# Output products of 13 tiles of layer 1 put off to the end of the kernel

## The chip, the cores and the metric

The kernel runs on one core of a Trainium2 chip. The metric is the time of one execution on the device in microseconds (us); lower is better. "PE" is the matrix engine (TensorE), "DVE" the vector engine, "ACT" the scalar engine, "POOL" GpSimd and "SP" the engine whose queue issues the DMAs.

## What is computed

The input is x, 2048 rows of 512 numbers in float32. Two kinds of layer alternate, twice each:

```python
x = x + A(layernorm(x)); x = x + B(layernorm(x))      # layer 0 of the kernel
x = x + A(layernorm(x)); x = x + B(layernorm(x))      # layer 1 of the kernel

def A(x):   # Fourier mixing: real part of a transform over features and rows
    a, b = x @ dft_hid_re.T, x @ dft_hid_im.T
    return dft_seq_re @ a - dft_seq_im @ b            # 2048 x 2048 matrices

def B(x):   # experts looked up by product keys: 32 heads, 16 + 16 keys, 256 experts
    q = einsum("nd,dhc->nhc", x, w_q)
    s1, s2 = q[..., :128] @ k1.T, q[..., 128:] @ k2.T # 16 scores each, per head
    # the best 2 of each, the best 2 of their 4 sums: 2 experts e with gates g (softmax)
    act = gelu(einsum("nd,nhkd->nhk", x, u[e]))
    return einsum("nhk,nhk,nhkd->nd", g, act, v[e])
```

## The kernel before

**Layout.** The 2048 rows are 16 tiles of 128. Float32 products are made exact enough by splitting each operand into a rounded high part and the remaining low part (`xh` and `xl` for the normalized x), so that one product is three matmuls: high by high, high by low, low by high.

**Stages.** Each layer has nine units of rows: units 0 to 6 have two tiles each, units 7 and 8 one tile. `ORDER` lists them; in layer 1 it is 0, 7, 1, 2, 3, 4, 5, 6, 8. For each unit, `seq_unit` (matmuls of L510) multiplies all 16 blocks of normalized x by that unit's blocks of the row transform. The blocks come by DMA (`raw`, L446), are split by ACT (L450) and DVE (L454), and the sum of the 16 steps lies in four accumulators `acc`. The sum is split into `pth` and `ptl` (L535, L538). The mark `xfree[s]` is the last use of block s of x.

Then `token_tile` works through each tile of the unit:

- the feature transform (L607), the add of the row (L617) and the layernorm;
- turning the normalized row over. For the tiles marked by `MOVED` (the first 13 of layer 1 among them), DVE turns 32x32 blocks (L659), the result goes to DRAM (L663), and four DMAs bring back pieces with the blocks in turned order, in runs of 32 numbers (L672). For other tiles PE transposes (L691);
- the scores (L721, L725) and the products with all 256 rows of u (L752);
- top-two selection by chains of maximum and comparison on DVE (L811 to L916), for 32 heads at a time;
- the gates, built as a 128 x 256 matrix: comparisons on DVE (L956, L962), small matmuls (L972), an ACT copy (L982), out to DRAM in four DMAs (`gdr`, L1002) and back in two (`gt` or, for the last tile, `raw`, L1010), because the values change partitions on the way;
- p, the product of gates and gelu (L1012). PE turns p (L1020), ACT and DVE split it into `ph` and `pl` (L1024, L1028), and six matmuls of 128x512 multiply it by the 256 rows of v, `vh` and `vl` (L1039, L1043). DVE adds the result to the row (L1054), and SP stores the row (L1059 in layer 1).

**What sets the order.** All this is written as operations given to a planner (`Plan`). Each has an engine, an assumed duration, its predecessors, the buffers that it takes (`take`) and gives back (`last`), and a priority. The planner takes operations in order of the time at which they could start, and among those that could start first the one with the lowest priority tuple. The operations are then issued in order of planned start, so that the order on each engine is fixed. Token work (priority 0) comes before sequence products (priority 5). For the last tile (tile 15, unit 8; `FINAL`, `fine`) an operation is also preferred when it could start within `SLACK` = 0.14 us of the first. A DMA is planned with at most eight (`LANES`) on the way. On SP the planner takes 0.3 us for one of the four turned pieces and 1.05 us for 256 KB.

When the last sequence product has been planned and a gap on PE of over 1.0 us remains, filler matmuls whose result isn't used are put into it (L1123).

```python
            elif free >= seq_last.start and gap > 1.0:
                for _ in range(int((gap - 0.4) / MM512)):
                    fill(1)
```

The functions that the diff touches:

Of the kernel before, what the change touches and what calls it, by code (L numbers as in the profile page):

```python
# [8 lines left out]
F32 = mybir.dt.float32  # L9
F32R = mybir.dt.float32r  # L10
# [18 lines left out]
E = 16  # L29
N = E * E  # L30
# [13 lines left out]
def MOVED(layer, at):  # L44
    return at >= 2 if layer == 0 else at < NCH + NSC * (TPC - 1) - 2


FILL0 = 10
FIRST = 4
LANES = 8  # L50
# [19 lines left out]
class Plan:  # L70
# [77 lines left out]
MM512, MM256, TR32, TR16, MMG = 0.230, 0.121, 0.110, 0.057, 0.026  # L148


def dve(n, rate=1):
    return 0.069 + n / (0.96e3 * rate)


def act(n):
    return 0.09 + n / 1.2e3


def load(kb):
    return kb / 256 * 1.05  # L160
# [3 lines left out]
def spectral_peer_kernel(ctx: ExitStack, tc, x_in, cseq, ctile, dhid, wq, k1t, k2t, ut, vm, out):  # L164
    nc = tc.nc
# [6 lines left out]


    BUFS = {"acc": 4, "bank": 4, "raw": 4, "c": 3, "p": 1, "row": 4, "wr": 5, "wp": 2,
            "tok": 3, "sc": 1, "eq": 1, "act": 3, "q": 2, "top": 1, "qt": 1, "lr": 4, "gt": 1, "pp": 1, "gdr": 2, "xdr": 2, "bn": 1}
    plan = Plan(BUFS)


    xh = const.tile([P, NT, D], F32R, name="xh")
    xl = const.tile([P, NT, D], F32R, name="xl")  # L180
    dh = const.tile([P, 2, KD, D], F32R, name="dh")
    dl = const.tile([P, 2, KD, D], F32R, name="dl")
    wh = const.tile([P, KD, 2, H, E], F32R, name="wh")
# [3 lines left out]
    vh = const.tile([P, 2, D], F32R, name="vh")  # L187
# [74 lines left out]
    def ln_apply(dst, src, i):  # L262
        nc.scalar.activation(dst, src, AF.Identity, bias=stats[:, i, 2:3], scale=stats[:, i, 1:2])
# [5 lines left out]

    def xhat(layer, i, get, after, take, last, prio):  # L270
        if layer == 0 and i < FIRST:
            b = xhigh[i] = op("ACT", act(512) + 0.18, lambda: ln_apply(xh[:, i, :], get(), i), after, take=take, prio=prio)
            a = op("ACT", act(512) + 0.18, lambda: ln_apply(get(), get(), i), [b], prio=prio)
            xready[layer, i] = op("DVE", dve(512), lambda: nc.vector.tensor_sub(xl[:, i, :], get(), as32(xh[:, i, :])),
                                  [a], last=last, prio=prio)
            return
        a = op("ACT", act(512) + 0.18, lambda: ln_apply(get(), get(), i), after, take=take, prio=prio)
        b = op("ACT", act(512), lambda: nc.scalar.copy(xh[:, i, :], get()), [a], prio=prio)
        xready[layer, i] = op("DVE", dve(512), lambda: nc.vector.tensor_sub(xl[:, i, :], get(), as32(xh[:, i, :])),
                              [b], last=last, prio=prio)  # L280

    xload = {}
# [143 lines left out]
    def seq_unit(layer, at, n, banks="acc"):  # L426
# [42 lines left out]
        def target(d):  # L469
            if b is None:  # L470
                return acc[d].rearrange("p c t -> p (c t)")
            return acc[d // 2][:, d % 2]

        for s0 in range(0, NT, 2):
            for s in (s0, s0 + 1):
                if s % per == 0:
                    pieces[s // per] = piece(s // per)

            steps = [(d, s) for s in (s0, s0 + 1) for d in range(KD)]
            if layer == 0 and at == 0 and s0 < FIRST:  # L480

                for s in (s0, s0 + 1):
                    ready, hc, moving = pieces[s]

                    def f(s=s, moving=moving, parts=(0, 1)):
                        for d in range(KD):
                            if s == 0:
                                acc[d] = psum.tile([P, 2, T], F32, name=banks, bufs=BUFS[banks])
                            for part in parts:
                                nc.tensor.matmul(target(d), xh[:, s, d * P:(d + 1) * P], moving(0, part),  # L490
                                                 start=(s == 0 and part == 0), stop=False, skip_group_check=True)

                    def g(s=s, moving=moving):
                        for d in range(KD):
                            nc.tensor.matmul(target(d), xl[:, s, d * P:(d + 1) * P], moving(0, 0),
                                             start=False, stop=False, skip_group_check=True)

                    seq_last = op("PE", 2 * KD * MM512, f, [ready, xhigh[s], seq_last], take=hold if s == 0 else [], prio=rank)
                    seq_last = xfree[s] = op("PE", KD * MM512, g, [xready[layer, s], seq_last], last=[hc], prio=rank)
                yield  # L500
                continue
            for d, s in sorted(steps) if s0 == NT - 2 else steps:
                ready, hc, moving = pieces[s // per]

                def f(s=s, d=d, moving=moving):
                    if s == 0 and d % blocks == 0:
                        shape = [P, 2, T] if b is None else [P, 2, 2, P]
                        acc[d // blocks] = psum.tile(shape, F32, name=banks, bufs=BUFS[banks])
                    for k, (w, part) in enumerate(((xh, 0), (xl, 0), (xh, 1))):
                        nc.tensor.matmul(target(d), w[:, s, d * P:(d + 1) * P], moving(s % per, part),  # L510
                                         start=(s == 0 and k == 0 and d % blocks == 0),
                                         stop=(s == NT - 1 and k == 2), skip_group_check=True)

                final = d == KD - 1 and s % per == per - 1
                seq_last = op("PE", 3 * (MM512 if b is None else MM256), f,
                              [ready, xready[layer, s], seq_last],
                              take=[hold[d // blocks]] if s == 0 and d % blocks == 0 else [],
                              last=[hc] if final else [], prio=rank)
                if d == KD - 1:
                    xfree[s] = seq_last  # L520
                    if s == NT - 4:
                        near[layer, n] = seq_last
                done[d] = seq_last
            yield
# [24 lines left out]
                parts[d] = firsts[-1], a  # L549


    x2done = {}
    last = {}
    stores = []
# [2 lines left out]
    def token_tile(layer, n, i, t0, at):  # L557
# [2 lines left out]
        late = (0, layer, at, i, 1)  # L560
        fine = prio[:3] == FINAL
        moved = MOVED(layer, at)
        hrow = Hold("row")
        t = {}

# [60 lines left out]
            a = ln_stats(lambda: t["row"], i, [b] + ([xready[1, i]] if (1, i) in xready else []), prio)  # L626


        hx, hxb = Hold("tok"), Hold("lr")
        ks = [slice(0, KD)] if not fine else [slice(0, KD // 2), slice(KD // 2, KD)]  # L630
        xn = []

        def f_xn(z, k):
            def f():
                if z == 0:
                    t["xn"] = work([P, D], F32, "tok")
                cs = slice(k.start * P, k.stop * P)
                if z == 0:
                    ln_apply(t["xn"][:, cs], t["row"][:, cs], i)
                else:  # L640
                    nc.vector.tensor_scalar(t["xn"][:, cs], t["row"][:, cs], stats[:, i, 1:2], stats[:, i, 2:3],
                                            op0=ALU.mult, op1=ALU.add)
            return f

        for z, k in enumerate(ks):
            w = (k.stop - k.start) * P
            xn.append(op("DVE", dve(w), f_xn(z, k), [a], behind=xn, prio=prio) if z else
                      op("ACT", act(w) + 0.18, f_xn(z, k), [a] + setup_done, take=[hx], prio=prio))

        hth, htl = Hold("tok"), Hold("tok")  # L650
        a_th, a_tl = [], []
# [354 lines left out]
        for j in range(2):  # L1006
            def f_in(j=j):
# [2 lines left out]
                nc.sync.dma_start(t["gt"][j * 64:(j + 1) * 64], t["gdr"][j].rearrange("e t g f -> (t g) e f"))  # L1010
            back.append(op("SP", 0.4, f_in, moves, behind=back, take=[hgt] if j == 0 else [], last=[hd], prio=prio, lag=3.5))
        a = op("DVE", dve(N), lambda: nc.vector.tensor_mul(t["act"], t["act"], t["gt"].rearrange("p e f -> p (e f)")),  # L1012
               back + [a_act], last=[hgt], prio=prio)

        hb, hpp = Hold("bank"), Hold("pp")

        def f_pt():
            t["pt"] = bank([P, 2, P])
# [1 line left out]
                nc.tensor.transpose(t["pt"][:, k, :], t["act"][:, k * P:(k + 1) * P], identf)  # L1020

        def f_ph():
            t["ph"] = work([P, 2, P], F32R, "ph", "pp")
            nc.scalar.copy(t["ph"], t["pt"])  # L1024

        def f_pl():
            t["pl"] = work([P, 2, P], F32R, "pl", "pp")
            nc.vector.tensor_sub(t["pl"], t["pt"], as32(t["ph"]))  # L1028

        a = op("PE", 2 * TR32, f_pt, [a], take=[hb], last=[hact], prio=prio)  # L1030
# [76 lines left out]

    for layer in range(2):
        mix(layer)

    order = sorted(plan.run(), key=lambda o: o.start)

# [64 lines left out]
```

## Time and profile before

| | |
|---|---|
| median of 3 runs | 1273.01 us (1272.3 to 1273.83) |
| the profiled execution, its own time | 1273.94 us |
| its span, first to last instruction | 1272.2 us |
| busy PE / DVE / ACT / POOL | 98% / 79% / 37% / 4% of the span |
| mean granted PE clock | 0.998 of full speed |
| moved by DMA | 134.55 MB, mean 106 GB/s |

The profiled execution is one run; its time contains about 1.7 us around the span. Times in the rows of the profile are microseconds from the span's start. A matmul's duration contains its way through the array and overlaps the next one's, so a PE that is 98% busy is not at its peak; how close two matmuls follow each other is read from the chain that ended last, in order of time. "Idle before, released by" names what an instruction had waited for.

### The profile page before, as it was taken

What the parts mean: (1) busy time and instruction counts of PE and PEld (TensorE: products, weight loads), DVE (VectorE), ACT (ScalarE), POOL (GpSimd) and SP (SyncE); (2) the same over time, 40 slices, a digit from 0 to 9 for tenths busy, and PEclk for the clock granted to TensorE, in tenths of its full rate; (3) what the DMA queues carried; (4) which work ended last, traced back from release to release, by engine and by line L of the source; (5) the groups of instructions that cost most, each with busy time, mean ns of one, the idle gap of its engine ahead of it and who ended that gap; (6) DMA issues with size and microseconds to landing.
All of it is one profiled execution on the core that took longest, in us unless ns stands there. A gap on an engine that the chain in (4) does not pass through costs nothing.

```text
span 1272.2 us, 20722 instructions
## 1 busy us (share of the span) xinstructions
PE 1251.6 (98%) x7686; PEld 1033.4 (81%) x7686; DVE 1007.7 (79%) x2277; ACT 466.6 (37%) x968; POOL 46.7 (4%) x71
## 2 busy tenths in 40 slices
PE   9999999999999999999999999999999999999997
PEld 6877778777787888899889887887888888888985
DVE  8899998899896877769885498595686849686784
ACT  7522143343333333334563233333333333333411
POOL 2000000000100000000000000000000000000000
PEclk9999999999999999999999999999999999999999
DMA  7866540342525242442554223424243342424002
GB/s 237 270 193 212 191 150 27 86 102 69 117 66 120 80 91 80 100 113 72 134 151 134 82 67 90 109 67 119 73 99 101 83 116 74 116 59 100 26 10 42
DMA packets 284693, 134.55 MB, mean 106 GB/s; under 512 B 193840, under 2 KB 259888, under 8 KB 284592
## 3 DMA queue, kind: packets, MB, share of 16 engines
q1 hardware_dynamic: 284592, 133.23, 39.1%
q8 instruction: 60, 0.98, 0.3%
q14 instruction: 41, 0.34, 0.1%
HBM read 114.05 MB, written 19.14 MB: 105 GB/s over the span
## 4 chain that ended last, share of the span: by engine, by line
PE 71%; DVE 14%; issue 5%; DMA 5%; ACT 2%; SPq 2%; POOL 1%; POOLq 0%; DVEq 0%; ACTq 0%
PE acc L510 40%; PE bank L607 10%; PE bank L721 7%; PE bank L725 3%; PE bank L752 3%; PE bank L1039 2%; DVE cl L454 2%; PE bank L510 2%; PE bank L384 1%; DMA tok<-xdr 1%; DVE eq L805 1%; DVE w L376 1%; DMA raw<-x2d 1%; PE bank L972 1%; PE bank L1043 1%
## 5 line engine op out<-in xcount | busy, mean ns | idle before, releaser
L510 PE MATMUL acc<-ch,xh 128*128 128x512 f32 (+1 forms) x1072 | 405.7, 378 | 0.2 <-DVE ptl L538 0.2
L510 PE MATMUL acc<-cl,xh 128*128 128x512 f32 (+1 forms) x1072 | 397.6, 371 | 0.0
L510 PE MATMUL acc<-ch,xl 128*128 128x512 f32 (+1 forms) x1072 | 397.4, 371 | 0.0
L450 ACT CAST ch<-raw 128x512 fp32r<-128x512 f32 x256 | 158.3, 619 | 284.9 <-PE acc L510 228.3
L510 PEld LDWEIGHTS acc<-cl,xh 128*128 128x128 f32 x1072 | 202.0, 188 | 35.6
L510 PEld LDWEIGHTS acc<-ch,xh 128*128 128x128 f32 x1072 | 202.2, 189 | 33.3 <-DVE ptl L538 1.0
L510 PEld LDWEIGHTS acc<-ch,xl 128*128 128x128 f32 x1072 | 202.4, 189 | 31.4
L454 DVE TENSOR_TENSOR cl<-raw,ch 128x512 fp32r<-128x512 f32 x256 | 174.5, 684 | 57.2 <-ACT ch L450 54.4
L607 PE MATMUL bank<-dh,pth 128*128 128x512 f32 (+1 forms) x264 | 103.3, 394 | 0.7 <-ACT pth L535 0.7
L721 PE MATMUL bank<-wh,tok 128*128 128x512 f32 x256 | 100.6, 393 | 1.0 <-ACT tok L679 0.7
L607 PE MATMUL bank<-dl,pth 128*128 128x512 f32 (+1 forms) x264 | 100.8, 384 | 0.0
L721 PE MATMUL bank<-wl,tok 128*128 128x512 f32 x256 | 99.8, 390 | 0.0
L607 PE MATMUL bank<-dh,ptl 128*128 128x512 f32 (+1 forms) x264 | 95.9, 384 | 0.1
L811 DVE TENSOR_TENSOR tmp<-sc 128x512 f32<-128x512 f32 (+1 forms) x66 | 44.3, 672 | 64.9 <-ACT sc L730 64.3
L956 DVE TENSOR_TENSOR lr<-iota,qt 128x1024 f16<-128x1024 f16 x124 | 80.0, 684 | 10.9 <-ACT qt L937 10.9
L252 POOL TENSOR_TENSOR stats<-stats,half 128x1 f32<-128x1 f32 x64 | 45.4, 714 | 1176.6 <-DVE stats L249 1095.3
L730 ACT COPY sc<-bank 128x512 f32<-128x512 f32 x64 | 36.4, 588 | 134.0 <-PE bank L725 73.8
L805 DVE TENSOR_TENSOR eq<-sc,val 128x1024 f16<-128x1024 f32 (+1 forms) x66 | 78.6, 1191 | 1.8
L725 PE MATMUL bank<-wh,tok 128*128 128x512 f32 x256 | 68.5, 389 | 0.0
L829 DVE TENSOR_TENSOR eq<-eq 128x256 f16<-128x256 f16 (+3 forms) x198 | 60.1, 303 | 1.4
L535 ACT CAST pth<-acc 128x512 fp32r<-128x512 f32 x62 | 36.4, 587 | 60.1 <-PE acc L510 57.1
L607 PEld LDWEIGHTS bank<-dh,pth 128*128 128x128 f32 x264 | 49.7, 188 | 10.5 <-ACT pth L535 1.0
(140 smaller groups left out, 1809.0 us busy)
## 6 DMA issues: line engine op xcount, KB each, us to landing
raw<-in_cseq SPq DMA_DIRECT2D x224, 256.0 KB, 2.8
wr<-in_wq SPq DMA_DIRECT2D x32, 512.0 KB, 3.8
raw<-in_ctile SPq DMA_DIRECT2D x32, 256.0 KB, 2.8
xdr<-lr SPq DMA_DIRECT2D x25, 256.0 KB, 2.2
tok<-xdr SPq DMA_DIRECT2D x100, 64.0 KB, 2.6
wr<-in_x SPq DMA_DIRECT2D x16, 256.0 KB, 3.4
row<-in_x SPq DMA_DIRECT2D x16, 256.0 KB, 3.6
x2d<-row SPq DMA_DIRECT2D x16, 256.0 KB, 2.2
```

Of the source, the lines that this page charges most:

```text
L252: nc.gpsimd.tensor_tensor(st[:, 1:2], st[:, 1:2], half, op=ALU.pow)
L450: nc.scalar.copy(t[1], t[0])
L454: nc.vector.tensor_sub(t[2], t[0], as32(t[1]))
L510: nc.tensor.matmul(target(d), w[:, s, d * P:(d + 1) * P], moving(s % per, part), start=(s == 0 and k == 0 and d % blocks == 0), stop=(s == ...
L607: nc.tensor.matmul(t["y", cs.start], w[:, k, c, t0:t0 + P], r[:, c, k, cs], start=(z == 0 and c == 0 and m == 0), stop=(z == len(steps) - ...
L721: nc.tensor.matmul(t["pc", hf], t["th"][:, k, :], r[:, k, hf], start=(k == 0 and r is wh), stop=False)
L725: nc.tensor.matmul(t["pc", hf], t["tl"][:, k, :], wh[:, k, hf], start=False, stop=(k == KD - 1))
L752: nc.tensor.matmul(t["xu"], w[:, k, :], r[:, k, :], start=(m == 0), stop=(m == 3 * KD - 1))
L805: nc.vector.tensor_tensor(t["eq"][:, :, cols], flat("sc")[:, :, cols], val(rank_, cols), op=ALU.is_equal)
L811: nc.vector.tensor_max(t["tmp"][:, :, cols], flat("sc")[:, :8, cols], flat("sc")[:, 8:, cols])
L829: nc.vector.tensor_max(s[:, :m], s[:, :m], s[:, m:2 * m])
L956: nc.vector.tensor_tensor(t["m", hf, r], io2, row_of(r, hf), op=ALU.is_equal)
```

## The change

For the 13 tiles of layer 1 in units 0, 7 and 1 to 5 (`DEFERRED`), the product of p and v is no longer made when p is there.

- After the feature transform's add, the row is stored in DRAM (`xod`), and its buffer is given back once the normalization has read it.
- DVE turns p in 32x32 blocks (into the buffer of the gates, `gt`), ACT and DVE split it there into high and low part in one buffer `pp`, and one DMA stores both in DRAM (`ptd`). PE's two transposes of p go.
- At the end, for each of the 13 tiles (`off`), once block z of x has been used for the last time, four DMAs bring p back, with the blocks in turned order, into the buffer of that block's `xl`; ACT copies it into the buffer of `xh` as matmul operand; the row is loaded over it. After the last sequence product, six matmuls into an `acc` bank follow, ACT copies the result out (into one of three buffers of `xg`), DVE adds it to the row, and SP stores the row. Priority (9, z) is behind everything else. At most three tiles have a bank at a time (`late`), and three an evicted result (`ev`).
- To make this possible, `xh` and `xl` become 16 separate tiles each, of 13 and 3 buffers.
- Tiles 12, 13 (unit 6) and 15 (unit 8) are worked as before, with `ph` and `pl` now lying in one buffer.

```diff
+def DEFERRED(layer, at):
+    return layer == 1 and at < NCH + NSC * (TPC - 1) - 2
+LATE = 13
...
-            "tok": 3, ..., "gdr": 2, "xdr": 2, "bn": 1}
+            "tok": 3, ..., "gdr": 2, "xdr": 2, "late": 3, "ev": 3, "bn": 1}
...
-    xh = const.tile([P, NT, D], F32R, name="xh")
-    xl = const.tile([P, NT, D], F32R, name="xl")
+    xh = [const.tile([P, D], F32R, name=m, bufs=b) for m, b in (("xh", LATE), ("xg", NT - LATE)) for _ in range(b)]
+    xl = [const.tile([P, D], F32R, name=m, bufs=b) for m, b in (("xl", LATE), ("xm", NT - LATE)) for _ in range(b)]
...
+    xod = dram.tile([NT, P, D], F32, name="xod")
+    ptd = dram.tile([NT, 4, 32, 2, 2, 4, 32], F32, name="ptd")
+    put_off = []
+    turn, cast = [], []
+
+    def off(z, i, stored, kept):
+        hb, hv, t = Hold("late"), Hold("ev"), {}
+        prio = (9, z)
+        a0 = []
+        for j in range(4):
+            def f_in(j=j):
+                if j == 0:
+                    t["row"] = const.tile([P, D], F32, name="xl", bufs=LATE)
+                nc.sync.dma_start(t["row"][32 * j:32 * j + 32].rearrange("p (b i t) -> p b i t", i=4, t=32),
+                                  ptd[i][:, :, :, :, j, :].rearrange("i d a k t -> d (a k) i t"))
+            a0.append(op("SP", 0.3, f_in, [stored, xfree[z]], behind=a0[-1:] or turn[-1:], prio=prio, lag=3.0))
+        turn.append(a0[-1])
+
+        def f_w():
+            t["w"] = const.tile([P, 2, 2, P], F32R, name="xh", bufs=LATE)
+            nc.scalar.copy(t["w"].rearrange("p a k t -> p (a k t)"), t["row"])
+
+        a0 = [op("ACT", act(512), f_w, a0, behind=cast[-1:], prio=prio)]
+        cast.extend(a0)
+        a1 = op("SP", load(256), lambda: nc.sync.dma_start(t["row"], xod[i]), a0 + [kept], prio=prio, lag=2.3)
+        a = None
+        for n, (part, k, r) in enumerate([(0, 0, vh), (0, 0, vl), (0, 1, vh), (0, 1, vl), (1, 0, vh), (1, 1, vh)]):
+            def f(n=n, part=part, k=k, r=r):
+                if n == 0:
+                    t["po"] = psum.tile([P, D], F32, name="acc", bufs=BUFS["acc"])
+                nc.tensor.matmul(t["po"], t["w"][:, part, k], r[:, k, :], start=(n == 0), stop=(n == 5))
+            a = op("PE", MM512, f, a0 + [a, seq_last], take=[hb] if n == 0 else [], prio=prio + (n,))
+
+        def f_ev():
+            t["ev"] = const.tile([P, D], F32, name="xg", bufs=NT - LATE)
+            nc.scalar.copy(t["ev"], t["po"])
+
+        a = op("ACT", act(512), f_ev, [a], take=[hv], last=[hb], prio=prio)
+        a = op("DVE", dve(512), lambda: nc.vector.tensor_add(t["row"], t["row"], t["ev"]), [a, a1], last=[hv], prio=prio)
+        op("SP", load(256), lambda: nc.sync.dma_start(out[i * P:(i + 1) * P, :], t["row"]), [a], prio=prio, lag=2.3)
...
+        if deferred:
+            kept = op("SP", load(256), lambda: nc.sync.dma_start(xod[i], t["row"]), [b], last=[hrow], prio=prio, lag=2.3)
...
+        if deferred:
+            def f_turn():
+                nc.vector.transpose(t["gt"].rearrange("p e f -> p (e f)"), t["act"])
+            def f_high():
+                t["pp"] = work([P, 2, N], F32R, "pp")
+                nc.scalar.copy(t["pp"][:, 0], t["gt"].rearrange("p e f -> p (e f)"))
+            def f_low():
+                nc.vector.tensor_sub(t["pp"][:, 1], t["gt"].rearrange("p e f -> p (e f)"), as32(t["pp"][:, 0]))
+            def f_keep():
+                nc.sync.dma_start(ptd[i].rearrange("i d a k j t -> (i d) (a k j t)"), as32(t["pp"]).rearrange("p a n -> p (a n)"))
+            a = op("DVE", dve(N), f_turn, [a], last=[hact], prio=prio)
+            a = op("ACT", act(N) + 0.05, f_high, [a], take=[hpp], prio=prio)
+            a = op("DVE", dve(N), f_low, [a], last=[hgt], prio=prio)
+            put_off.append((i, op("SP", load(256), f_keep, [a], last=[hpp], prio=prio, lag=2.3), kept))
+            return
...
     for layer in range(2):
         mix(layer)
+    for z, parts in enumerate(put_off):
+        off(z, *parts)
```

More of the change, by code (lines that the diff above doesn't have):

```diff
@@ L174, in spectral_peer_kernel @@
     BUFS = {"acc": 4, "bank": 4, "raw": 4, "c": 3, "p": 1, "row": 4, "wr": 5, "wp": 2,
-            "tok": 3, "sc": 1, "eq": 1, "act": 3, "q": 2, "top": 1, "qt": 1, "lr": 4, "gt": 1, "pp": 1, "gdr": 2, "xdr": 2, "bn": 1}
+            "tok": 3, "sc": 1, "eq": 1, "act": 3, "q": 2, "top": 1, "qt": 1, "lr": 4, "gt": 1, "pp": 1, "gdr": 2, "xdr": 2, "late": 3, "ev": 3, "bn": 1}
     plan = Plan(BUFS)
-    xh = const.tile([P, NT, D], F32R, name="xh")
-    xl = const.tile([P, NT, D], F32R, name="xl")
+    xh = [const.tile([P, D], F32R, name=m, bufs=b) for m, b in (("xh", LATE), ("xg", NT - LATE)) for _ in range(b)]
+    xl = [const.tile([P, D], F32R, name=m, bufs=b) for m, b in (("xl", LATE), ("xm", NT - LATE)) for _ in range(b)]
     dh = const.tile([P, 2, KD, D], F32R, name="dh")
@@ L271, in xhat @@
         if layer == 0 and i < FIRST:
-            b = xhigh[i] = op("ACT", act(512) + 0.18, lambda: ln_apply(xh[:, i, :], get(), i), after, take=take, prio=prio)
+            b = xhigh[i] = op("ACT", act(512) + 0.18, lambda: ln_apply(xh[i], get(), i), after, take=take, prio=prio)
             a = op("ACT", act(512) + 0.18, lambda: ln_apply(get(), get(), i), [b], prio=prio)
-            xready[layer, i] = op("DVE", dve(512), lambda: nc.vector.tensor_sub(xl[:, i, :], get(), as32(xh[:, i, :])),
+            xready[layer, i] = op("DVE", dve(512), lambda: nc.vector.tensor_sub(xl[i], get(), as32(xh[i])),
                                   [a], last=last, prio=prio)
@@ L277, in xhat @@
         a = op("ACT", act(512) + 0.18, lambda: ln_apply(get(), get(), i), after, take=take, prio=prio)
-        b = op("ACT", act(512), lambda: nc.scalar.copy(xh[:, i, :], get()), [a], prio=prio)
-        xready[layer, i] = op("DVE", dve(512), lambda: nc.vector.tensor_sub(xl[:, i, :], get(), as32(xh[:, i, :])),
+        b = op("ACT", act(512), lambda: nc.scalar.copy(xh[i], get()), [a], prio=prio)
+        xready[layer, i] = op("DVE", dve(512), lambda: nc.vector.tensor_sub(xl[i], get(), as32(xh[i])),
                               [b], last=last, prio=prio)
@@ L489, in f @@
                             for part in parts:
-                                nc.tensor.matmul(target(d), xh[:, s, d * P:(d + 1) * P], moving(0, part),
+                                nc.tensor.matmul(target(d), xh[s][:, d * P:(d + 1) * P], moving(0, part),
                                                  start=(s == 0 and part == 0), stop=False, skip_group_check=True)
@@ L494, in g @@
                         for d in range(KD):
-                            nc.tensor.matmul(target(d), xl[:, s, d * P:(d + 1) * P], moving(0, 0),
+                            nc.tensor.matmul(target(d), xl[s][:, d * P:(d + 1) * P], moving(0, 0),
                                              start=False, stop=False, skip_group_check=True)
@@ L509, in f @@
                     for k, (w, part) in enumerate(((xh, 0), (xl, 0), (xh, 1))):
-                        nc.tensor.matmul(target(d), w[:, s, d * P:(d + 1) * P], moving(s % per, part),
+                        nc.tensor.matmul(target(d), w[s][:, d * P:(d + 1) * P], moving(s % per, part),
                                          start=(s == 0 and k == 0 and d % blocks == 0),
@@ L562, in token_tile @@
         moved = MOVED(layer, at)
+        deferred = DEFERRED(layer, at)
         hrow = Hold("row")
@@ L626, in token_tile @@
             a = ln_stats(lambda: t["row"], i, [b] + ([xready[1, i]] if (1, i) in xready else []), prio)
+        kept = None
+        if deferred:
+            kept = op("SP", load(256), lambda: nc.sync.dma_start(xod[i], t["row"]), [b], last=[hrow], prio=prio, lag=2.3)
         hx, hxb = Hold("tok"), Hold("lr")
@@ L647, in token_tile @@
             xn.append(op("DVE", dve(w), f_xn(z, k), [a], behind=xn, prio=prio) if z else
-                      op("ACT", act(w) + 0.18, f_xn(z, k), [a] + setup_done, take=[hx], prio=prio))
+                      op("ACT", act(w) + 0.18, f_xn(z, k), [a] + setup_done, take=[hx], last=[hrow] if deferred else [], prio=prio))
         hth, htl = Hold("tok"), Hold("tok")
@@ L1012, in token_tile @@
         a = op("DVE", dve(N), lambda: nc.vector.tensor_mul(t["act"], t["act"], t["gt"].rearrange("p e f -> p (e f)")),
-               back + [a_act], last=[hgt], prio=prio)
+               back + [a_act], last=[] if deferred else [hgt], prio=prio)
         hb, hpp = Hold("bank"), Hold("pp")
+        if deferred:
[13 more added lines that the diff above has]
+            return
         def f_pt():
@@ L1022, in f_ph @@
         def f_ph():
-            t["ph"] = work([P, 2, P], F32R, "ph", "pp")
+            t["pp"] = work([P, 2, N], F32R, "pp")
+            t["ph"], t["pl"] = (t["pp"][:, m].rearrange("p (k t) -> p k t", t=P) for m in range(2))
             nc.scalar.copy(t["ph"], t["pt"])
         def f_pl():
-            t["pl"] = work([P, 2, P], F32R, "pl", "pp")
             nc.vector.tensor_sub(t["pl"], t["pt"], as32(t["ph"]))
```

## The prediction, made before the change was run

> **What bounds the kernel now.** I read the page first, then busy time by stage, then the chain that ended last, then the queue of SyncE in the tail.
>
> ```profile
> span 1272.2 us, 20722 instructions
> PE 1251.6 (98%) x7686; PEld 1033.4 (81%) x7686; DVE 1007.7 (79%) x2277; ACT 466.6 (37%) x968; POOL 46.7 (4%) x71
> ```
> ```profile
> 620.00:1000.00 380.00, 378.59 (x2119) 313.89 (x2118) 279.88 (x638) 144.02 (x295) 8.87 (x13) 1.00 0.38 99
> 1000.00:1150.00 150.00, 150.00 (x809) 123.22 (x808) 109.98 (x250) 51.93 (x109) 2.17 (x4) 1.00 0.36 93
> ...
> 1158.00:1176.00 18.00, 18.00 (x119) 14.99 (x118) 8.36 (x15) 4.06 (x8) 0.00 (x0) 1.00 0.41 88
> 1176.00:1199.00 23.00, 23.00 (x146) 20.77 (x145) 13.85 (x32) 7.65 (x15) 1.07 (x2) 1.00 0.15 38
> 1199.00:1215.30 16.30, 16.25 (x162) 15.81 (x160) 15.92 (x43) 5.94 (x15) 0.00 (x0) 1.00 0.00 1
> 1215.30:1249.20 33.90, 30.43 (x188) 24.95 (x188) 30.59 (x99) 8.15 (x21) 0.93 (x1) 1.00 0.08 9
> 1249.20:1263.40 14.20, 11.38 (x73) 8.37 (x72) 4.95 (x11) 3.09 (x9) 0.00 (x0) 0.89 0.39 53
> 1263.40:1272.20 8.80, 4.93 (x22) 3.54 (x20) 1.54 (x3) 0.38 (x1) 0.00 (x0) 0.89 0.22 65
> ```
> The columns are the stretch, its length, then busy PE, weight load, DVE, ACT, POOL, then the granted clock, DMA share and GB/s. Layer 1 runs from about 640. In the stretches up to 1215.3, where the last sequence product ends, PE stands idle for under 2 us in all, while DVE is 74% busy (279.88 of 380, 109.98 of 150). So up to 1215.3 each microsecond of PE work costs one. After 1215.3 the last tile (tile 15) runs alone through its token work, and there PE is filled up:
>
> ```profile
> L1123 PE MATMUL acc<-dh x104: 387/389/628, 1221.3 to 1266.5; 128*128 128x512 f32 x104
> ```
> These are the 104 filler matmuls, whose result nobody reads. The tail's order is that of DVE, then of two DMA round trips:
>
> ```profile
> 1183.17 0.43 SPq L568 DMA_DIRECT2D row<-x2d  x1
> 1222.86 2.64 SPq L1002 DMA_DIRECT2D gdr<-sc  x4
> 1227.06 1.32 SPq L1010 DMA_DIRECT2D gt<-gdr  x2
> 1249.25 2.63 SPq L1002 DMA_DIRECT2D gdr<-pth  x4
> 1254.73 1.32 SPq L1010 DMA_DIRECT2D raw<-gdr  x2
> 1256.14 0.62 SPq L1002 DMA_DIRECT2D gdr<-sc  x1
> ...
> 1257.47 1.99 SPq L1002 DMA_DIRECT2D gdr<-sc  x3
> 1261.05 1.32 SPq L1010 DMA_DIRECT2D gt<-gdr  x2
> ```
> ```profile
> 1258.54 0.43 DVE L1012 TENSOR_TENSOR act<-act,raw 128x256 f32<-128x256 f32 x1 [3.96 <-DMA raw<-gdr]
> ...
> 1268.37 0.69 DVE L1054 TENSOR_TENSOR row<-row,bank 128x512 f32<-128x512 f32 x1 [1.30 <-PE bank L1043]
> ```
> Tile 15's gates leave at 1249.25 and return for the product at 1258.54. Tile 13's go out behind them on SP (1256.14 to 1262.4), so tile 13, not tile 15, ends last, with its add at 1268.37.
>
> **The change part by part.** What one put-off tile takes off PE, from the chain in order of time, where entries are spaced by issue and not by overlapping durations:
>
> ```profile
> 1103.56 0.23 PE bank L1020 x2
> ...
> 1105.87 0.93 PE bank L1039 x4
> 1106.80 0.47 PE bank L1043 x2
> ```
> (1) Two transposes and six products go: 0.23 + 0.93 + 0.47 = 1.63 us a tile, 21.2 us for 13. All 13 tiles (units 0, 7, 1 to 5) have their products before 1215.3, the last of them in the stretches from 1158 on, where PE is still busy throughout. What fills PE there is the sequence product of unit 8, real work, so its end moves by the whole 21.2 us. Term: -21.2.
>
> (2) The six products return after that end: 13 x 1.40 = 18.2 us. Room on PE: the 104 fillers at the issue spacing 0.93 / 4 are 24.2 us, and idle time is 56.9 - (30.43 + 11.38 + 4.93) = 10.2 us; 34 us in all. Term 0. With that cover gone it costs 18.2.
>
> (3) Work around the put-off point in the steady part. DVE loses an add and gains a 128x256 transpose; ACT's cast and DVE's subtract stay, reading SBUF.
>
> ```profile
> L1054 DVE TENSOR_TENSOR row<-row,bank x32: 648/686/691, 244.0 to 1268.4; 128x512 f32<-128x512 f32 x32
> L659 DVE STREAM_TRANSPOSE lr<-tok x25: 674/711/715, 271.8 to 1104.1; 128x512 f32<-128x512 f32 x25
> SPq L1059 <- DVE row L1054: 33.2, 9, 7.4
> ```
> The transpose has half the elements of the one shown: estimate 0.36 us from that row, against 0.69 gone. SP issues two stores (row, p) for the one store removed. Each stands in SP's order until DVE has finished, and behind it stand the loads of sequence blocks. The store they replace already made SP wait up to 7.4 us while PE between 1000 and 1150 never paused. So 0, bounds 0 to +1 us. The buffers of p and of the gates are single, and are now held until the split, for p until its store lands: a few microseconds. Here is how far apart their users come within one pair of tiles:
>
> ```profile
> 1087.63 1.33 SPq L1010 DMA_DIRECT2D gt<-gdr  x2
> 1098.50 1.32 SPq L1010 DMA_DIRECT2D gt<-gdr  x2
> ```
> That is 10.9 us, so 0.
>
> (4) Loads on SP: per tile four pieces of p in 128-byte runs, then the row.
>
> ```profile
> L672 SPq DMA_DIRECT2D tok<-xdr x100: 568/634/1453, 274.5 to 1113.6; - x100
> L1059 SPq DMA_DIRECT2D out<-row x16: 338/362/1316, 780.6 to 1269.1; - x16
> GB/s 237 270 193 212 191 150 27 86 102 69 117 66 120 80 91 80 100 113 72 134 151 134 82 67 90 109 67 119 73 99 101 83 116 74 116 59 100 26 10 42
> ```
> Four times 0.634 (same shape) plus 0.36 is 2.9 us a tile, 37.7 us for 13. They start as each block of x is used up for the last time, spread over unit 8's sequence product (about 1176 to 1215). SP issues nothing between 1183.6 and 1222.86 and between 1228.4 and 1249.25, 60 us. Before tile 15's scores at 1225.72 (row further down) PE wants at most three of them, by the room from the first filler at 1221.3: 4.4 us for 1.40 each. Term 0; if the queue lags, 37.7 in 60 still leaves nothing ahead of tile 15's gates at 1249.25.
>
> (5) In the tail DVE gets 13 adds of 0.686, 8.9 us, and ACT 26 casts. DVE is dense until 1249.2 (30.59 of 33.9) and idle 9.25 + 7.26 = 16.5 us afterwards, so most adds fit there. The planner lets tile 15's operations go first only when they come within 0.14 us, so an add or a cast can stand before one of them. Bounds 0 to +8.9; I take +2, about three such hits, since the row nearest is the idle time, which exceeds the adds.
>
> (6) 13 stores of 256 KB. At the highest rate of the GB/s row, 270, one takes 0.97 us, 12.6 us in all. Three eviction buffers and a dense DVE hold some ten of them back until DVE is free at 1249, which is where the two gate round trips run. Bounds 0 to +12.6; I take +3, between, nearer to 0 because these 14 us have a DMA share of 0.39 only.
>
> ```profile
> gdr<-sc SPq DMA_DIRECT2D x124, 32.0 KB, 2.2
> ...
> DMA to landing us min/median/max: 2.1/2.2/5.0
> ```
> Gates going out land in 2.2 us in the median, over a layer with DMA share 0.37, and in 5.0 at worst. The Trainium skill ("DMA: Bandwidth & Descriptors", Latency and other measured facts) speaks against the change here: it puts memory latency at 0.2 us on average and 2 us at high load. By it each of the two landings in tile 15's path would grow by up to 1.8 us, and the sum with 3.6 in place of 3 would be 0.6 later. The median row does not show it at this load; only the 5.0 does.
>
> Sum, against the profiled execution: its span is 1272.2 and its time 1273.94. 1273.94 - 21.2 + 2 + 3 = 1257.7. The median of the runs, 1273.01, is 0.9 lower, which gives 1256.8: **1257 us**.
>
> **The rivals.**
> *A: the tail gives back half.* All 13 stores stand before tile 13's gates, at 12.6 us, and the hits of (5) add 2: 1273.0 - 21.2 + 14.6 = 1266.4, band 1262 to 1270. For it: tile 13 is already last, and stands on SP behind others. Against: SP needs only 0.36 us for a store, and three buffers let the first go early.
>
> *B: the products aren't covered.* They run only after tile 15, as a block: 18.2 of the 21.2 returns, then one add and one landing, 0.69 + 2.4 by the row below, come behind: 1273.0 - 21.2 + 18.2 + 3.1 = 1273.1, no change. Against: 34 us of room on PE.
>
> ```profile
> out<-row SPq DMA_DIRECT2D x16, 256.0 KB, 2.4
> 1225.72 2.12 PE bank L721 x8
> 1227.84 0.93 PE bank L725 x4
> ...
> 1259.99 1.81 PE bank L1039 x4
> ```
> ```profile
> 1259.12 0.41 PE L1020 MATMUL bank<-identf,act 128*128 128x128 f32 x2 [1.79 <-DVE act L1012]
> ```
> *C: slower.* Late adds stand in DVE's fixed order ahead of tile 15's top-two selection and wait for their products. One such stop costs the six products and an eviction, 1.40 + 0.62 (ACT's mean 128x512 cast, row below) = 2.0 us; 13 stops are 26: 1273.0 - 21.2 + 26 = 1278. It decides from 1.63 us a tile. For it: each engine's order is fixed by planned times. Against: DVE's plan is dense there, and prefers tile 15.
>
> ```profile
> L450 ACT CAST ch<-raw 128x512 fp32r<-128x512 f32 x256 | 158.3, 619 | 284.9 <-PE acc L510 228.3
> ```
> *D: a cold clock.* Fillers wait for nothing; late products wait for loads and evictions. The four products at 1259.99, after idle time on PE and fewer matmuls, took 1.81 us where 1105.87 shows 0.93, and the granted clock of that stretch is 0.89. If PE stalls so ahead of 1225.72, tile 15's first scores (2.12 + 0.93) take twice as long, +3.1, and with a stall of about 3 us the result is 1263. The Trainium skill ("TensorE: Matmul & The Clock Gate", What's actually happening) says that the array falls to half rate after about one idle window of 3.4 us. The trace agrees with the halving; the idle time that it shows just ahead, 1.79 us before 1259.12, is shorter than that window. Against: the fill routine still puts fillers into gaps over 1 us.
>
> **How the numbers follow.** Forecast (1250 to 1261) 0.67; A 0.17; D 0.05; B 0.04; C 0.05; more than forecast (below 1250) 0.02. A measurement tells about 0.2%, 2.5 us. Faster: 0.67 + 0.17 + 0.05 + 0.02 = 0.91; same 0.04; slower 0.05. Low end 1250: terms (5) and (6) at zero give 1251.8, less 1.4 for PE's idle time between 620 and 1000, which may go, 1250.4. High end 1266: (5) at 2 and (6) at 12.6. Outside lie B, C, half of A and the 0.02: 0.2.
>
> **What would show it.** Matmuls of 128x512 from p with the values' matrix, 78 of them, after the last sequence product, and far fewer than 104 fillers; that last sequence product ending near 1194; PE without idle time in layer 1. (5) is wrong if DVE's stretch from tile 15's first score products to its gates (1225.72 to 1249.25, 23.5 us) grows by over 2 us; (6) is wrong if the time from tile 15's gates leaving to the end (23 us) grows by other than about 3. The prediction fails if PE waits behind a late product ahead of tile 15's work, or if sequence blocks come late behind the new stores.

## The result: 1257.7 us, the forecast sum, with three of its terms wrong

| | median | range | ratio to before, with 95% interval |
|---|---|---|---|
| before | 1273.42 us | 1272.3 to 1274.1 (4 runs) | |
| 13 tiles put off | 1257.7 us | 1256.32 to 1259.73 (4 runs) | 0.9879 (0.9862 to 0.9896) |

The profiled execution of the changed kernel took 1259.73 us, the longest of the four, with a span of 1257.7; the spans compared below contain these 2 us. All times given are of fast runs: one slow run of e3 (1728.22 us, granted clock 0.655) and one slow run of the kernel before (4379.56 us) are left out. The head of the page, the late products (`acc<-vh,xh` and `acc<-vl,xh`, 52 + 26 = 78 as forecast) and the fillers that are left (45 of 104):

```profile
span 1257.7 us, 20768 instructions
PE 1234.3 (98%) x7601; PEld 1019.9 (81%) x7601; DVE 1011.2 (80%) x2290; ACT 481.3 (38%) x994; POOL 46.4 (4%) x71
...
L588 PE MATMUL acc<-vh,xh x52: 387/389/628, 1201.1 to 1245.6; 128*128 128x512 f32 x52
L588 PE MATMUL acc<-vl,xh x26: 387/389/628, 1201.5 to 1245.0; 128*128 128x512 f32 x26
L1198 PE MATMUL acc<-dh x45: 387/389/501, 1227.5 to 1252.1; 128*128 128x512 f32 x45
```
Busy time by stage of the changed kernel (stretch, length, busy PE, weight load, DVE, ACT, POOL, granted clock, DMA share, GB/s):

```profile
1000.00:1150.00 150.00, 149.59 (x831) 122.85 (x830) 111.66 (x255) 54.05 (x114) 2.19 (x4) 1.00 0.41 105
...
1150.00:1176.00 26.00, 26.00 (x154) 23.10 (x153) 13.51 (x30) 10.62 (x21) 1.06 (x2) 1.00 0.62 133
1176.00:1203.50 27.50, 22.28 (x195) 21.15 (x195) 23.56 (x56) 10.64 (x24) 0.00 (x0) 0.95 0.68 141
1203.50:1236.20 32.70, 31.09 (x192) 25.95 (x192) 28.24 (x96) 11.87 (x28) 0.55 (x1) 0.99 0.28 67
1236.20:1250.00 13.80, 13.00 (x86) 9.73 (x85) 11.02 (x21) 6.65 (x15) 0.00 (x0) 1.00 0.69 154
1250.00:1257.70 7.70, 3.93 (x18) 2.57 (x16) 1.54 (x3) 0.37 (x1) 0.00 (x0) 1.00 0.62 234
```
One row was not forecast: from 1176 to 1203.5, where the kernel before has a full PE, PE stands idle for 5.2 us. The waits on PE in the last 160 us (us in total, times, longest), then ACT and PE around that place, in order of time:

```profile
PE bank L656 <- ACT pth L540: 3.6, 1, 3.6
PE bank L986 <- DVE q L953: 2.1, 3, 1.6
PE bank L1025 <- DVE cl L1015: 1.3, 2, 0.9
```
```profile
1198.05 0.62 ACT L578 CAST xh<-xl 128x512 fp32r<-128x512 f32 x1 [4.15 <-DMA xl<-ptd]
1198.57 0.58 ACT L540 CAST pth<-acc 128x512 fp32r<-128x512 f32 x1
1201.20 0.62 ACT L578 CAST xh<-xl 128x512 fp32r<-128x512 f32 x1 [2.05 <-DMA xl<-ptd]
1201.73 0.58 ACT L540 CAST pth<-acc 128x512 fp32r<-128x512 f32 x1
```
```profile
1195.31 0.28 PE L515 MATMUL acc<-cl,xg 128*128 128x256 f32 x1
1199.20 0.39 PE L656 MATMUL bank<-dh,pth 128*128 128x256 f32 x1 [3.62 <-ACT pth L540]
...
1201.55 0.63 PE L588 MATMUL acc<-vl,xh 128*128 128x512 f32 x1
1201.98 0.63 PE L588 MATMUL acc<-vh,xh 128*128 128x512 f32 x1
```
The first part of tile 15's sum is ready on PE at 1195.6. Its copy `pth` (L540) stands on ACT behind a returning cast of p (L578), and that waits 4.15 us for its load. PE waits 3.62 us for `pth`, and soon after runs at half speed: two late products start 0.43 us apart, where 0.93 / 4 = 0.23 is the pace that the prediction read. The chain that ended last goes through the same places:

```profile
1193.83 0.63 SPq L571
1194.50 3.48 DMA xl<-ptd
1198.05 0.62 ACT xh L578
1198.66 0.49 ACT pth L540
1199.20 1.21 PE bank L656 x8
```
Ahead of these rows it is SP's issues, one behind the other, from 1184.86 on. Between 1179 and 1200 SP waits for other engines for 1.2 us in all; the rest is issuing.

The other 1.6 of the 5.2 us are a second hit of the same kind, on tile 12. Returning casts that wait stand on ACT ahead of a step of tile 12's gelu (L821), DVE waits 1.82 us for that, its selection ends later (by 1.9 us against e1, counted from layer 0's last store), and PE waits for tile 12's keys (ACT, DVE and PE, one block each):

```profile
1171.39 0.62 ACT L578 CAST xh<-xl 128x512 fp32r<-128x512 f32 x1 [2.53 <-DMA xl<-ptd]
...
1173.31 0.62 ACT L578 CAST xh<-xl 128x512 fp32r<-128x512 f32 x1 [0.57 <-DMA xl<-ptd]
1173.84 0.41 ACT L821 ACTIVATE act<-act 128x256 f32<-128x256 f32 x1
```
```profile
1174.28 0.43 DVE L822 TENSOR_TENSOR act<-act 128x256 f32<-128x256 f32 x1 [1.82 <-ACT act L821]
```
```profile
1186.45 0.37 PE L986 MATMUL bank<-ident,q 128*128 128x128 f16 x3 [1.61 <-DVE q L953]
```

### The profile page after: what moved, and what is told of

The parts are those of the page before. It is cut to its first block, busy times and chain, and to the rows that moved or that the text cites. A ratio compares the mean times of both kernels' runs of the same rounds, so it can differ in the third digit from the quotient of the medians.

```text
span 1257.7 us, 20768 instructions
## 1 busy us (share of the span) xinstructions
PE 1234.3 (98%) x7601; PEld 1019.9 (81%) x7601; DVE 1011.2 (80%) x2290; ACT 481.3 (38%) x994; POOL 46.4 (4%) x71
## 4 chain that ended last, share of the span: by engine, by line
PE 77%; DVE 14%; DMA 3%; issue 2%; SPq 2%; ACT 1%; POOL 1%; DVEq 0%; ACTq 0%
PE acc L515 40%; PE bank L656 11%; PE bank L774 8%; PE bank L778 4%; PE bank L805 3%; DVE cl L459 2%; PE bank L515 2%; DVE w L381 1%; PE bank L1112 1%; PE bank L389 1%; PE bank L1025 1%; DMA raw<-x2d 1%; DVE eq L882 1%; DVE eq L858 1%; PE acc L588 1%
## 5 line engine op out<-in xcount | busy, mean ns | idle before, releaser
L515 PE MATMUL acc<-ch,xh 128*128 128x512 f32 (+1 forms) x868 | 328.5, 378 | 0.2 <-DVE ptl L543 0.2
L515 PE MATMUL acc<-ch,xl 128*128 128x512 f32 (+1 forms) x868 | 321.8, 371 | 0.0
L515 PE MATMUL acc<-cl,xh 128*128 128x512 f32 (+1 forms) x868 | 321.8, 371 | 0.0
L515 PEld LDWEIGHTS acc<-cl,xh 128*128 128x128 f32 x868 | 163.5, 188 | 28.6
L515 PEld LDWEIGHTS acc<-ch,xh 128*128 128x128 f32 x868 | 163.7, 189 | 27.2 <-DVE ptl L543 1.1
L515 PEld LDWEIGHTS acc<-ch,xl 128*128 128x128 f32 x868 | 163.9, 189 | 25.2
L783 ACT COPY sc<-bank 128x512 f32<-128x512 f32 x64 | 36.3, 588 | 134.0 <-PE bank L778 65.2
L515 PE MATMUL acc<-ch,xg 128*128 128x512 f32 (+1 forms) x204 | 77.4, 380 | 0.0
L515 PE MATMUL acc<-cl,xg 128*128 128x512 f32 (+1 forms) x204 | 75.9, 372 | 0.0
L515 PE MATMUL acc<-ch,xm 128*128 128x512 f32 (+1 forms) x204 | 75.7, 371 | 0.0
```

The costliest lines, as they stand in the source:

```text
L515: nc.tensor.matmul(target(d), w[s][:, d * P:(d + 1) * P], moving(s % per, part), start=(s == 0 and k == 0 and d % blocks == 0), stop=(s == ...
L783: nc.scalar.copy(t["sc"][:, :, hf, :], t["pc", hf].rearrange("p h e -> p e h"))
```

## What the runs told apart

Theory 1: the planned order on ACT puts returning casts ahead of tile 15's copies, because the planner takes 0.3 us on SP for a piece that takes 0.634; the steady part gains what the prediction said. Theory 2: the returning work itself holds tile 15 up, in any order.

**e1: the true SP time for returning pieces.**

```diff
-            a0.append(op("SP", 0.3, f_in, [stored, xfree[z]], ...
+            a0.append(op("SP", 0.65, f_in, [stored, xfree[z]], ...
```


> Only the planner's assumed time on SP for one returning piece of p is changed, 0.3 to 0.65 us (the trace of the changed kernel shows 0.634), so only the orders differ. Theory 1 (ACT's fixed order puts returning casts of p ahead of tile 15's casts pth, and they wait for loads that SP issues later than planned; PE waits 3.6 us for pth): the wait goes, tile 15 starts some 5 us earlier, 1252 us (1250 to 1254). Theory 2 (tile 15's start is held by the late products and their transfers themselves, whatever the order): 1256 to 1259.

Measured: 1251.99 us, ratio 0.9828 (0.9812 to 0.9845). Only the orders differ, so theory 2 falls. ACT, and the stretch that had 5.2 us of idle PE:

```profile
1190.17 0.62 ACT L578 CAST xh<-xl 128x512 fp32r<-128x512 f32 x1 [4.49 <-DMA xl<-ptd]
1191.51 0.59 ACT L540 CAST pth<-acc 128x512 fp32r<-128x512 f32 x1 [0.72 <-PE acc L515]
```
```profile
1176.00:1203.50 27.50, 27.50 (x238) 25.85 (x237) 26.69 (x75) 14.02 (x31) 0.57 (x1) 1.00 0.61 122
```
A cast still waits 4.49 us for its load, but ends before tile 15's sum is ready; now `pth` waits for PE, and the clock stays at 1.00. The wait for tile 12's keys is down to 0.3 us at most.

**e2: nothing returns.** The call of `off` is left out.

```diff
-    for z, parts in enumerate(put_off):
-        off(z, *parts)
```


> The 13 put-off products never return: no loads, casts, products, adds and stores at the end (13 tiles of the output are not written). Theory 1 (steady part gains the whole 21.2 us, the return costs some 6 us, nearly all of it ahead of tile 15): 1252 us (1250.5 to 1253.5). Theory 2 (the steady part gains only some 15 us, because new stores and DVE work take the rest, and the return is free): 1257 to 1259.

Measured: 1244.87 us, 0.9768 (0.9754 to 0.9783). Lower than both theories said. Tile 15's first scores divide the difference (before, in the prediction: 1225.72); the rows are the changed kernel, e1 and e2, one each:

```profile
1212.77 0.43 PE L774 MATMUL bank<-wh,tok 128*128 128x512 f32 x1
```
```profile
1204.05 0.40 PE L774 MATMUL bank<-wh,tok 128*128 128x512 f32 x1
```
```profile
1204.08 0.50 PE L774 MATMUL bank<-wh,tok 128*128 128x512 f32 x1
```
Up to there e1 and e2 agree within 0.03 us (0.3 us when counted from layer 0's last store): with the right order the return costs nothing ahead of tile 15's scores. Their difference lies at the end: from tile 15's gates (`gdr<-pth`) to the end it is 15.7 us in e2 and 21.4 in e1. In e2 tile 13's gates (`gdr<-sc`) leave before tile 15's (`gdr<-pth`); before the change, in the change and in e1 they leave after:

```profile
1223.89 2.62 SPq L1055 DMA_DIRECT2D gdr<-sc  x4
1227.49 2.60 SPq L1055 DMA_DIRECT2D gdr<-pth  x4
```
**e3: late casts planned behind `pth`.**

```diff
-        a0 = [op("ACT", act(512), f_w, a0, behind=cast[-1:], prio=prio)]
+        a0 = [op("ACT", act(512), f_w, a0, behind=cast[-1:] + ([pready[1, 8][KD - 1][0]] if z >= 4 else []), prio=prio)]
```


> The returning casts of p from the fifth tile on are planned behind tile 15's last cast pth; SP's loads stay early. Theory 1 (casts ahead of pth on ACT): PE's wait for pth is under 1 us and the time 1252 us (1250 to 1255; nine casts of 0.62 then stand near tile 15's first steps). Theory 2 (late loads and products as such): 1256 to 1259.

Measured: 1253.08 us, 0.9833 (0.9812 to 0.9854). The wait for `pth` is gone while SP is planned as in the change, so ACT's order is the cause of that wait and not SP's queue in itself. A wait of 2.0 us for tile 12's keys remains, and so do the first four casts, which e3 doesn't move. Counted from layer 0's last store, tile 15's scores come 4.0 us earlier than in the change; e1 has 7.0.

**e4: p in one load, not turned.**

```diff
-        for j in range(4):
+        for j in range(1):
...
-                nc.sync.dma_start(t["row"][32 * j:32 * j + 32].rearrange(...), ptd[i][:, :, :, :, j, :].rearrange(...))
+                nc.sync.dma_start(t["row"], ptd[i].rearrange("i d a k j t -> (i d) (a k j t)"))
...
-            a0.append(op("SP", 0.3, f_in, ...
+            a0.append(op("SP", 0.38, f_in, ...
```


> Each tile's p returns in one DMA of 256 KB in place of four pieces of 64 KB (not turned over, so these 13 tiles get a wrong p): SP spends about 0.4 us a tile in place of 2.5, the bytes are the same. Theory 1, with SP's issue time as the reason for the late loads: no wait for pth, 1252 us (1250 to 1254). Rival (the loads are late because of the bytes or the landing, not the issue): 1256 to 1258.

Measured: 1251.86 us, 0.9821 (0.9806 to 0.9836), and no wait for `pth`. The same bytes in about a sixth of the issue time, landing no sooner (2.9 us in the median, against 2.7 a piece): so the bytes and the landing alone don't make the loads late. The edit also gives the planner the true time of the one load (0.38 us). It can't tell a shorter issue from a truer plan; e1 shows that the truer plan alone is enough.

**e9: seven tiles instead of 13** (units 0, 7, 1, 2; the planner at 0.3 us).

```diff
-    return layer == 1 and at < NCH + NSC * (TPC - 1) - 2
-LATE = 13
+    return layer == 1 and at < 4
+LATE = 7
```


> Only 7 tiles are put off (units 0, 7, 1, 2), with the planner's SP time of 0.3 us as in the change. Theory 1 (1.63 us of PE gained per tile; the loss ahead of tile 15 comes from SP falling behind by 0.34 us a piece, which grows with the number of tiles): 1273.4 - 7 x 1.63 = 1262, plus 0 to 1.5: 1261 to 1263.5, and PE's wait for tile 15's pth under 1 us. Rival (the loss is a fixed price of returning anything): 1267 to 1270.

Measured: 1267.05 us, 0.9947 (0.9930 to 0.9965). Theory 1's number missed: the loss did not shrink with the number of tiles. It has the same form at another place. Here a waiting cast stands ahead of the copy of tile 12's scores (L783), and PE waits for that tile's keys. Matmuls that started 0.12 us apart before start 0.21 apart after, for some 3 us:

```profile
1179.79 0.62 ACT L578 CAST xh<-xl 128x512 fp32r<-128x512 f32 x1 [4.19 <-DMA xl<-ptd]
1180.32 0.58 ACT L783 COPY sc<-bank 128x512 f32<-128x512 f32 x1
```
```profile
1194.83 0.28 PE L515 MATMUL acc<-ch,xm 128*128 128x256 f32 x1
1194.95 0.28 PE L515 MATMUL acc<-cl,xg 128*128 128x256 f32 x1
1197.44 0.47 PE L986 MATMUL bank<-ident,q 128*128 128x128 f16 x3 [2.21 <-DVE q L953]
...
1198.24 0.41 PE L515 MATMUL acc<-cl,xg 128*128 128x256 f32 x1
1198.45 0.41 PE L515 MATMUL acc<-ch,xg 128*128 128x256 f32 x1
```
**e10: seven tiles, with e1's 0.65 us.**

> Seven tiles put off as in e9, with the planner's true SP time of 0.65 us a piece. In e9 a returning cast held ACT for 4.2 us ahead of the copy of tile 12's scores, and PE then waited 2.2 us for tile 12's keys. Theory 1 (the loss is such a hit, and goes with the true SP time): 7 x 1.63 = 11.4 under before, 1262 us (1260.5 to 1263.5). Rival (a fixed price of returning anything, some 5 us): 1265.5 to 1268, as e9.

Measured: 1264.02 us, 0.9924 (0.9909 to 0.9939), half a microsecond above theory 1's band and 1.5 below the rival's. No fixed price of 5 us, then. Counted from layer 0's last store, tile 15's first scores come 11.6 us earlier than before, theory 1's 11.4; what is missing from its band lies behind tile 15's gates (24.1 us to the end, before 23.0). In these runs a loss was a hit on one or two instructions, or none, not a sum over tiles.

**e11: e1 without the 13 returning stores.**

```diff
-        op("SP", load(256), lambda: nc.sync.dma_start(out[i * P:(i + 1) * P, :], t["row"]), [a], prio=prio, lag=2.3)
```


> e1 without the 13 returning stores (those 13 tiles of the output are not written). Theory 1 (stores are hidden): 1251 to 1252.5, as e1. Rival (stores collide with the two gate round trips at the end, as the prediction had it): 3 us or more under e1, 1246 to 1249.

Measured: 1252.0 us, 0.9826 (0.9811 to 0.9841); e1 had 1251.99. The stores cost nothing.

**e7b and e7: tile 13's gates first.** e7b is e1 with tile 15's first scores planned behind the turning of tile 13's keys (`turned13` holds that operation). e7 also plans the returning adds behind tile 13's last selection step.

```diff
-                              take=[] if z else [hb], prio=prio)
+                              take=[] if z else [hb], behind=[] if z or hf else turned13, prio=prio)
```


> The true SP time as in e1, and one more planned order: tile 15's first score products come behind the turning of tile 13's keys on PE, so that tile 13's gates can leave before tile 15's. In e2, where nothing returns, that order came about by itself and the time from tile 15's gates to the end was 15.7 us, against 21.4 in e1. Theory 1 (the remaining 6 to 7 us between e1 and e2 are this order, the return itself is free): 1246 us (1244 to 1248.5). Rival (they are the price of the 13 stores and adds at the end): 1251 to 1253, as e1.

> As e7b, and the 13 returning adds are planned behind tile 13's last selection step on DVE. Theory 1: 1246 us, and within 1.5 us of e7b, since the early adds number only three. Rival (early adds are what throws tile 13 back): 2 us or more under e7b. Second rival (adds pushed together at the end cost time): 1249 to 1252.

Measured: 1249.11 us, 0.9803 (0.9787 to 0.9818), and 1248.94 us, 0.9801 (0.9786 to 0.9817). That order gives 2.9 us, not 6, and when the adds come makes no difference. In e7b tile 15's scores start at 1205.43, 1.4 us later than in e1, because they wait for tile 13. Some 4 us to e2 remain. Counted from layer 0's last store, 2.2 of them lie ahead of tile 15's first scores, 0.5 between scores and gates, 1.0 behind the gates; what causes them was not settled.

**e8: the kernel before with that order.**

> The kernel before, with tile 15's first scores behind the turning of tile 13's keys; nothing is put off. If the order at the end is worth 6 us by itself and has nothing to do with what is put off: 1268 us (1266 to 1270). Rival (the kernel before has no slack there, tile 15 waits as long as tile 13 gains): 1272 to 1276.

Measured: 1270.79 us, 0.9970 (0.9958 to 0.9981): 3 us, half of what was expected and as much as in e7b. So those 3 us need nothing put off.

**e12b: the true SP time for all small DMAs,** in e1; **e13: the same three edits in the kernel before.**

```diff
-                back.append(op("SP", 0.3, f_in, [b], ...            # turned rows
+                back.append(op("SP", 0.65, f_in, [b], ...
-            moves.append(op("SP", 0.3, f_out, ...                   # gates out
+            moves.append(op("SP", 0.65, f_out, ...
-            back.append(op("SP", 0.4, f_in, moves, ...              # gates back
+            back.append(op("SP", 0.65, f_in, moves, ...
```


> All small DMAs get the SP time that the trace shows (0.65 us in place of 0.3 and 0.4: gates out and back, turned rows, returning p). In the planned order tile 13's keys are now turned ahead of tile 15's scores without being told to. Theory 1 (the orders suffer from the planner's SP times): 1247 to 1249.5, as e7. Rival (only the returning pieces mattered): 1251 to 1253, as e1.

> The kernel before with the planner's true SP time for all small DMAs; nothing is put off. e12b reached the end of layer 0 some 5 us earlier than the others (PE busy 318.9 of 320 us between 300 and 620, against 314.4 before) and had tile 13's gates ahead of tile 15's. If both are orders that need nothing put off: 1273.9 - 5 - 3 = 1266 us (1264 to 1268), and putting off is then worth 25 us beside it (e12b's 1241 against 1266). Rival (e12b's gain needs what is put off): 1271 to 1275.

Measured: e12b 1241.14 us, 0.9742 (0.9726 to 0.9758), 6 us under the best expectation and the fastest of all; e13 1267.47 us, 0.9955 (0.9938 to 0.9972). Both gain near the turn of the layers, outside what is put off. Busy time there, of e12b and of the kernel before:

```profile
300.00:620.00 320.00, 318.88 (x1949) 269.32 (x1949) 261.54 (x632) 122.02 (x261) 13.12 (x19) 1.00 0.39 94
```
```profile
300.00:620.00 320.00, 314.36 (x1925) 264.64 (x1924) 259.76 (x623) 117.80 (x254) 11.99 (x19) 1.00 0.37 92
```
Between these two, putting off 13 tiles goes with 1267.5 - 1241.1 = 26.3 us, against 15.7 between the first two kernels. Not all of it is the work put off: up to tile 15's gates, counted from layer 0's last store, e12b is 21.8 us ahead of e13, close to the forecast 21.2. Behind the gates it is another 5.1 ahead (17.9 us to the end, against 23.0), and there tile 13's gates leave first in e12b and last in e13. And e13's number lay in its band for one of the two reasons given only: layer 0's last store comes at 686.46, 5.9 us earlier than before, but the 3 us from tile 13's order did not come.

## Why the prediction was right, point by point

The sum held (1257 against 1257.7), but by errors that cancel: 7.3 us were lost at a place where the forecast had nothing, and the 5 us that it had put at the end did not come. The mechanism of the gain was right; that the total came out was luck. Here are the times of three marks (tile 15's first scores, its gates, the end), with the last store of layer 0 (`x2d<-row`), ahead of all that was put off, to take out where each execution stood by then; first before, then changed:

```profile
692.38 0.34 SPq L1064 DMA_DIRECT2D x2d<-row  x1
```
```profile
693.72 0.34 SPq L1137 DMA_DIRECT2D x2d<-row  x1
```
```profile
1236.21 2.64 SPq L1055 DMA_DIRECT2D gdr<-pth  x4
...
1242.48 2.67 SPq L1055 DMA_DIRECT2D gdr<-sc  x4
...
1254.68 0.33 SPq L1132 DMA_DIRECT2D out<-row  x1
```
- *Term (1), -21.2: right.* e2's first scores of tile 15 come 1225.72 - 1204.08 = 21.6 us earlier than before, and both kernels stand at 692.3 to 692.4 at layer 0's last store.
- *Term (2), 0: right.* 78 products took the place of 59 fillers and of idle time; e1 and e2 agree at tile 15's scores.
- *Term (3), 0: right.* PE is busy for 149.59 of 150 us from 1000 to 1150 with the new stores.
- *Term (4), 0: wrong; it is the step that failed.* From before to the change, tile 15's scores moved by 1225.72 - 1212.77 = 12.95, by 14.3 after the 1.3 us of layer 0. That is 7.3 short of 21.6. PE's 5.2 us of idle time are most of it; the slower pace is some 1.7 more (an estimate from the granted clocks: 5% of 27.5 us and 1% of 32.7). The sign that the prediction had set shows it too: the last sequence product was to end near 1194 and ended at 1201.3, and PE was to have no idle time in layer 1. The working counted SP's 37.7 us against 60 us of room, and asked when PE needs a load. It did not ask what stands behind the instruction that waits, on ACT: the cast, and behind it the steps of tiles 12 and 15. Term (5) did allow for casts ahead of tile 15's operations, but at their own length, not with a wait for a load. The condition was in sight (SP planned at 0.3 us, measured at 0.634).
- *Term (5), +2: wrong in size, within its bounds (0 to 8.9).* From tile 15's scores to its gates: 23.44 us, before 23.53. No late add starts in that stretch: three start before it, ten after the gates have left. Three late evictions on ACT stand in it and don't lengthen it.
- *Term (6), +3: wrong by the prediction's own sign.* From tile 15's gates to the end: 1257.7 - 1236.21 = 21.5, before 22.95; e11 shows no cost of the stores.
- Together: -21.6 + 7.3 - 0.1 - 1.5 + 1.3 = -14.6, and the spans differ by 14.5. The marks divide the span, so this must come out; what it tells is where each part lies.
- *Rival C* had the form that occurred (a late operation ahead of tile 15's, in a fixed order, waiting), but on DVE and for a product; on ACT and for a load it cost 7 us in two hits, not 26. *Rival D*'s stall of about 3 us and its halved pace followed from it, ahead of tile 15's scores as D had it, but the stall was for `pth` and not for a late product: 0.43 us between products after 3.62 us of idle PE, and a granted clock of 0.95 in the stretch. The Trainium skill ("TensorE: Matmul & The Clock Gate", What's actually happening) has half rate after about one idle window of 3.4 us; the trace of the changed kernel agrees, that of e9 doesn't (half pace after 2.21 us). *A and B* did not occur.
- The longer landings under load that the prediction weighed did not come. Tile 15's gates landed sooner than before, whose row has 2.8 us:

```profile
gdr<-pth SPq DMA_DIRECT2D x4, 32.0 KB, 2.1
```
The DMA share in the stretch of these four (1236.2 to 1241.1) was 0.46. Tile 13's four went out at a share of 0.75 (1242.4 to 1247) and landed in 2.2 us in the median, 2.6 at worst.

## What to carry to other kernels

Work moved off the path of the busiest engine brought here what its spacing on that engine said, and its return cost nothing ahead of the last tile's scores once the order was right. What the return does cost hung on the fixed order of another engine that it passes through, so for each waiting instruction that is added, ask what stands behind it there. In a kernel whose order is planned, a wrong assumed duration of one cheap step (0.3 us for 0.65) can cost more than the step: correcting four of them gained 16.6 us on top of the change (1257.7 to 1241.1), 6.6 of it ahead of layer 0's last store, where nothing is put off. A sum that comes out right is no proof of its terms; marks along the path are.

## What the runs showed of the hardware that was not expected

SP's issue, not the transfer, limited the returning loads:

```profile
L571 SPq DMA_DIRECT2D xl<-ptd x52: 562/634/1509, 1157.1 to 1204.4; - x52
```
Four pieces are 2.5 us of SP a tile, for the bytes that one issue of about 0.4 us moves in e4. The Trainium skill ("DMA: Bandwidth & Descriptors", Issuing engines are not separate DMA queues) calls the issue time usually small relative to the DMA itself. For one piece that is so here (0.634 against 2.7 us to landing); but the issues follow one another on SP, 33 us for the 52, and that queue is what the casts waited for.

The slow pace of PE came in e9 after 2.21 us of idle time, with PE dense before it, and lasted some 3 us; after 1.61 us of idle time in the changed kernel (at 1186.45) it did not come. Where between them it begins, and whether the length of the idle time alone decides, was not tested.
